# W1's loads in one queue, real B transposed and used first, the last 64 features in groups of 1,024 tokens, and the last columns in smaller pieces

## The chip, the cores and the metric

The kernel runs on one core of one Trainium2 chip. The metric is device time of one execution in microseconds (us). The execution's span in the trace is about 2 us shorter than that time; where a trace is read below, its span is quoted. All inputs are bf16.

## The reference

For x of 2,048 tokens by 640, the output is `g * a + (1 - g) * b`. `g` is a sigmoid gate per token, `a` is a diagonal state-space layer with 640 complex states, and `b` is a two-layer perceptron with 1,728 hidden features.

```python
Bu = einsum("bld,pd->blp", x, B_bar)              # B is complex: two real 640 x 640 matrices
for t in range(L):
    h = Lam_bar * h + Bu[:, t]                    # linear recurrence over the tokens
a = 2.0 * einsum("blp,dp->bld", hseq, C).real + x * Dskip     # C is complex too
b = gelu(x @ w1 + b1) @ w2 + b2                   # w1: 640 x 1728, w2: 1728 x 640
g = sigmoid((x * gate_w).sum(-1, keepdims=True))
```

The hidden features are 13 blocks of 128 and a last block of 64. That last block is one subject of the change.

## The kernel before

The tokens go in four quarters of 512. For each quarter TensorE does a hidden layer (`m1`), a B projection (`bproj`), then for each chunk of 128 tokens a second layer (`m2`) and a C projection (`cproj`). VectorE runs the recurrence as a scan, ScalarE does Gelu and takes results out of PSUM. Each engine's order comes from a small list scheduler inside the kernel, which uses estimated durations.

The first W1 columns come through the sync engine's queue (SPq), the rest in two loads from ScalarE's queue. The ten DMA transposes of B alternate between the real and the imaginary matrix and share one name, `"BT"`, so that the first projection waits for all ten:

```python
w1_rest(0, FW, NW2 * 128, "dtb")      # ScalarE's queue, 480 KB, after the first Exp
...
w1_rest(1, NW2 * 128, F, "sin")       # ScalarE's queue, 560 KB, after the sines
...
load_T("B", "l_B", [(BT[:, k, ci, :], (A_B_re, A_B_im)[ci][:, k * 128:(k + 1) * 128]) for k in range(KD) for ci in range(2)],
       ["BT"], prio=6.8, dur=13.1)
...
def bproj(q):
    for k in range(KP):
        for ci in range(2):           # real, imaginary, real, ...
            ...
            op(f"b_{q}_{k}{ci}", "pe", KD * d_mm(512), XT[q] + ["BT"], [("bank", bank)], f_mm, prio=pe_prio())
```

The last 64 features use half of the array's columns, so two halves of the quarter's tokens go to the two column halves, in every quarter:

```python
for k in range(KD):
    ...
    for h in range(2):                # n = 64 weights columns, 256 tokens each
        t = nc.tensor.matmul(PS[bank][h * 64:h * 64 + n, 0:256], W1sb[:, k, jf * 128:jf * 128 + n],
                             xT[:, k, q * 512 + h * 256:q * 512 + (h + 1) * 256], start=(k == 0), stop=(k == KD - 1))
```

The last chunk's C projection is two halves of 320 columns; after each, one VectorE operation adds everything up, and the half is stored.

## Time and profile before

218.64 us was the median of three runs (217.53 to 218.73).

| what | before |
|---|---|
| span of the traced run | 216.6 us |
| TensorE, VectorE, ScalarE busy | 98%, 88%, 46% |
| granted clock | 1.00 |
| chain from the first B projection to the last matmul | 21.70 to 213.92 us, TensorE alone |

The page's busy shares and its slices (40 equal slices of 5.4 us; a digit is the busy share in tenths) show an engine that is full and a DMA that is full only at the start:

```profile
PE 212.3 (98%) x1299; PEld 124.2 (57%) x1299; DVE 191.3 (88%) x268; ACT 100.2 (46%) x173; POOL 4.8 (2%) x14
...
PE   7999999999999999999999999999999999999995
...
DMA  6999499986300040000000013000000000000001
```

The chain of work that ended last, in order of time (start, us, what), follows the DMA issues on SPq, then the landing of the last imaginary transpose, then TensorE without a break:

```profile
16.75 4.91 DMA BT<-in_A_B_im_dram
21.66 0.05 issue
21.70 10.97 PE ps L690 x50
32.67 14.03 PE ps L658 x65
46.70 0.67 PE ps L662 x10
47.36 10.90 PE ps L690 x50
58.26 3.81 PE ps L765 x28
62.07 2.72 PE ps L789 x20
...
109.20 0.67 PE ps L662 x10
109.86 3.92 PE ps L765 x28
...
211.19 2.73 PE ps L789 x20
...
213.95 0.55 DVE osb L822
```

Three things are to be seen. 128x512 matmuls come every 216 ns (14.03 us / 65) and 128x320 ones every 136 ns (3.81 / 28). Each group of ten 64-column matmuls (line L662) takes 0.67 us, and the group after it is 0.11 us longer than its like elsewhere (3.92 against 3.81). And the first B projection (L690) starts on a DMA, not on TensorE. TensorE's own timeline shows the head and the hole there (start, duration, what, idle before it and what ended it):

```profile
5.17 0.94 PE L418 MATMUL ps<-ident,xn 128*128 128x128 bf16 x10
...
6.16 3.20 PE L637 MATMUL ps<-xT,W1sb 128*128 128x512 bf16 x14
...
20.52 0.74 PE L662 MATMUL ps<-xT,W1sb 128*64 128x256 bf16 x10
21.70 10.54 PE L690 MATMUL ps<-xT,BT 128*128 128x512 bf16 x48 [0.45 <-DMA BT<-in_A_B_im_dram]
```

### The profile page before, as it was taken

The numbers are of one execution on the slowest core, as the hardware profiler recorded it, in microseconds if no ns is written. First come the engines' busy times: TensorE is split into PE (matmuls) and PEld (weight loads), VectorE is DVE, ScalarE is ACT, GpSimd is POOL, SyncE is SP. The second block draws the span as 40 slices with busy tenths as digits, with TensorE's granted clock in tenths as the row PEclk, the third lists the DMA queues.
The fourth block names the chain that finished last, engine by engine and source line by source line (L and its number), as shares of the span: only waits on it lengthen the run. The fifth ranks groups of instructions, "written<-read, shape, count | busy, mean of one in ns | idle before, by whom it ended". The sixth has DMA issues, their size and how long they took to land.

```text
span 216.6 us, 3320 instructions
## 1 busy us (share of the span) xinstructions
PE 212.3 (98%) x1299; PEld 124.2 (57%) x1299; DVE 191.3 (88%) x268; ACT 100.2 (46%) x173; POOL 4.8 (2%) x14
## 2 busy tenths in 40 slices
PE   7999999999999999999999999999999999999995
PEld 3444444444577776444467777444457777777773
DVE  3899999999999999999997999799999989996312
ACT  2578556675533324556643233556673233232220
POOL 1010030000000100000000010000000000000000
PEclk9999999999999999999999999999999999999999
DMA  6999499986300040000000013000000000000001
GB/s 197 288 277 100 99 323 286 194 130 125 80 3 30 30 154 0 30 0 0 3 0 9 25 44 140 30 3 0 0 3 0 30 33 0 30 30 33 30 32 30
DMA packets 28858, 15.45 MB, mean 71 GB/s; under 512 B 22060, under 2 KB 28396, under 8 KB 28844
## 3 DMA queue, kind: packets, MB, share of 16 engines
q1 hardware_dynamic: 26912, 11.88, 23.5%
q0 software_dynamic: 560, 2.30, 3.5%
q10 hardware_dynamic: 1372, 1.07, 1.7%
q8 instruction: 10, 0.16, 0.3%
q14 instruction: 4, 0.03, 0.0%
HBM read 7.38 MB, written 2.62 MB: 46 GB/s over the span
## 4 chain that ended last, share of the span: by engine, by line
PE 89%; SPq 7%; DMA 2%; issue 0%; DVE 0%
PE ps L765 28%; PE ps L789 20%; PE ps L690 20%; PE ps L658 19%; SPq L335 6%; DMA BT<-in_A_B_im_dram 2%; SPq L328 1%; PE ps L662 1%; DVE osb L822 0%
## 5 line engine op out<-in xcount | busy, mean ns | idle before, releaser
L765 PE MATMUL ps<-W2sb,Gl 128*128 128x320 bf16 x448 | 63.6, 299 | 0.0
L765 PEld LDWEIGHTS ps<-W2sb,Gl 128*128 128x128 bf16 x448 | 43.6, 98 | 17.6 <-issue 0.4
L658 PE MATMUL ps<-xT,W1sb 128*128 128x512 bf16 x225 | 49.2, 379 | 0.0
L789 PE MATMUL ps<-CT,H 128*128 128x320 bf16 x320 | 46.1, 299 | 0.0
L730 DVE TENSOR_TENSOR_SCAN W<-atab,V 128x1280 bf16<-128x1280 f32 x16 | 44.3, 2812 | 0.3
L690 PE MATMUL ps<-xT,BT 128*128 128x512 bf16 x200 | 43.8, 379 | 0.4 <-DMA BT<-in_A_B_im_dram 0.4
L789 PEld LDWEIGHTS ps<-CT,H 128*128 128x128 bf16 x320 | 31.2, 98 | 12.3
L671 ACT ACTIVATE Gl<-ps,b1col 128x512 bf16<-128x512 f32 x45 | 30.6, 692 | 16.1 <-PE ps L658 16.1
L658 PEld LDWEIGHTS ps<-xT,W1sb 128*128 128x128 bf16 x225 | 22.0, 98 | 26.5
L690 PEld LDWEIGHTS ps<-xT,BT 128*128 128x128 bf16 x200 | 19.4, 98 | 23.7 <-DMA BT<-in_A_B_im_dram 0.7
L699 ACT ACTIVATE U<-ps 128x512 bf16<-128x512 f32 x40 | 23.9, 597 | 19.1 <-PE ps L690 19.1
L808 DVE SCALAR_TENSOR_TENSOR xg<-xn,gcol,dsk 128x640 bf16<-128x640 bf16 x16 | 13.9, 883 | 0.4
L773 ACT ACTIVATE E_0<-ps,g1col 128x320 bf16<-128x320 f32 x12 | 6.3, 527 | 16.5 <-PE ps L765 16.5
L616 DVE SCALAR_TENSOR_TENSOR scr<-xn,gwb 128x640 bf16<-128x640 bf16 x16 | 13.2, 823 | 0.4
L506 DVE TENSOR_TENSOR V<-V,W 128x1280 bf16<-128x1280 bf16 x16 | 12.5, 822 | 0.3
L506 DVE TENSOR_TENSOR H<-H,V 128x1280 bf16<-128x1280 bf16 x16 | 12.5, 822 | 0.3
L506 DVE TENSOR_TENSOR V<-mr,U 128x2560 bf16<-128x2560 bf16 x8 | 11.9, 1489 | 0.5 <-DVE s L506 0.3
L506 DVE TENSOR_TENSOR H<-c,W 128x2560 bf16<-128x2560 bf16 x8 | 11.9, 1488 | 0.1
L506 DVE TENSOR_TENSOR W<-mi,U 128x2560 bf16<-128x2560 bf16 x8 | 11.9, 1485 | 0.0
L506 DVE TENSOR_TENSOR V<-s,W 128x2560 bf16<-128x2560 bf16 x8 | 11.9, 1484 | 0.0
L773 ACT ACTIVATE E_2<-ps,g1col 128x320 bf16<-128x320 f32 x10 | 5.3, 527 | 13.4 <-PE ps L765 13.4
L773 ACT ACTIVATE E_1<-ps,g1col 128x320 bf16<-128x320 f32 x10 | 5.3, 528 | 13.3 <-PE ps L765 13.3
(95 smaller groups left out, 113.8 us busy)
## 6 DMA issues: line engine op xcount, KB each, us to landing
out_dram<-osb SPq DMA_DIRECT2D x15, 160.0 KB, 1.8
W2sb<-in_B_w_dram SPq DMA_DIRECT2D x1, 2080.0 KB, 12.7
xn<-in_A_x_dram POOLq DMA_DIRECT2D x3, 640.0 KB, 4.7
W1sb<-in_B_w_dram SPq DMA_DIRECT2D x5, 224.0 KB, 4.6
xn<-in_A_x_dram SPq DMA_DIRECT2D x2, 320.0 KB, 3.3
W1sb<-in_B_w_dram ACTq DMA_DIRECT2D x1, 560.0 KB, 5.2
W1sb<-in_B_w_dram ACTq DMA_DIRECT2D x1, 480.0 KB, 6.2
xT<-in_A_x_dram SPq DMA_TRANSPOSE x10, 4.0
```

Of the source, the lines that this page charges most:

```text
L335: t = dma_inc("sp", nc.sync.dma_start_transpose(dst, src), sem)
L506: return inc("dve", nc.vector.tensor_tensor(out=o, in0=a, in1=b, op=o_))
L616: t = inc("dve", nc.vector.scalar_tensor_tensor(out=scr[:, :], in0=xn[q % 2][:, c, :], scalar=1.0, in1=gwb[:, :], op0=ALU.mult, op1=ALU.mu ...
L658: t = nc.tensor.matmul(PS[bank][:, :], W1sb[:, k, jf * 128:(jf + 1) * 128], xT[:, k, q * 512:(q + 1) * 512], start=(k == 0), stop=(k == KD ...
L671: return inc("act", nc.scalar.activation(Gl[q % 2][:, jf, :], PS[bank][:, :], ACT.Gelu_apprx_tanh, bias=b1col[:, jf:jf + 1]))
L690: t = nc.tensor.matmul(PS[bank][:, :], BT[:, kd, ci, k * 128:(k + 1) * 128], xT[:, kd, q * 512:(q + 1) * 512], start=(kd == 0), stop=(kd = ...
L699: return inc("act", nc.scalar.activation(dst, src, ACT.Copy, scale=1.0 if ci == 0 else -1.0))
L730: t = inc("dve", nc.vector.tensor_tensor_scan(out=g[:, ci, :], data0=a, data1=v[:, ci, :], initial=0.0, op0=ALU.mult, op1=ALU.add))
L765: t = nc.tensor.matmul(PS[bank][:, 0:HALF], Gl[q % 2][0:n, jf, t4 * 128:(t4 + 1) * 128], W2sb[0:n, jf, cols], start=(jf == 0), stop=(jf == ...
L773: return inc("act", nc.scalar.activation(E1[c % NE][:, cols], PS[bank][:, 0:HALF], ACT.Copy, scale=g1col[:, c:c + 1]))
L789: t = nc.tensor.matmul(PS[bank][:, 0:HALF], H[b % NHB][:, ci, k, s * 128:(s + 1) * 128], CT[:, k, ci, cols], start=(i == 0), stop=(i == 2 ...
L808: return inc("dve", nc.vector.scalar_tensor_tensor(out=xg[c % 2][:, :], in0=xn[q % 2][:, c % 4, :], scalar=gcol[:, c:c + 1], in1=dsk[:, :] ...
```

## The change

The intent: TensorE is the bound, so take away its wait for B, make the 64-column groups fewer, and shorten what comes after the last matmul. The diff, cut to its core; left out are buffers, the banks' rotation, the second layer's last matmul reading the new buffer `GlL`, and the renaming of dependencies.

```diff
+        load("w1_r", "sp", "l_w1r", W1sb[:, :, FW:F], B_w1[:, FW:F].rearrange(...), [("w1", "r")], prio=6.5, lat=6.0)
...
-        w1_rest(0, FW, NW2 * 128, "dtb")
-        w1_rest(1, NW2 * 128, F, "sin")
...
-        load_T("B", "l_B", [(BT[:, k, ci, :], ...) for k in range(KD) for ci in range(2)], ["BT"], prio=6.8, dur=13.1)
+        for ci in range(2):
+            load_T(f"B{ci}", f"l_B{ci}", [(BT[:, k, ci, :], ...) for k in range(KD)], [("BT", ci)], prio=6.8 + 0.1 * ci, dur=6.6)
...
         def bproj(q):
-            for k in range(KP):
-                for ci in range(2):
+            for ci in range(2):
+                for k in range(KP):
...
+        def m1_last(q0):                      # the last 64 features of quarters q0 and q0 + 1
...
+                for k in range(KD):
+                    for h in range(2):
+                        t = nc.tensor.matmul(PS[bank][h * 64:(h + 1) * 64, :], W1sb[:, k, jf * 128:F],
+                                             xT[:, k, (q0 + h) * 512:(q0 + h + 1) * 512], start=(k == 0), stop=(k == KD - 1))
...
+        LAST = [(BK_C[0], 0, HALF), (BK_C[1], HALF, HALF + 192), (BK_M2[0], HALF + 192, D)]
...
         m1(1)
+        m1_last(0)
...
             m1(q)
+            if q % 2 == 0:
+                m1_last(q)
```

More of the change, by code (lines that the diff above doesn't have):

```diff
@@ L236, in bass_gated_mix__ssm_conv_s5__dense_activation_gelu__prompt_kernel @@
         CT = SB("CT", [128, KP, 2, D], BF16)
-        Gl = [SB(f"Gl_{i}", [128, NF, 512], BF16) for i in range(2)]
+        Gl = [SB(f"Gl_{i}", [128, NF - 1, 512], BF16) for i in range(2)]
+        GlL = [SB(f"GlL_{i}", [65, 512], BF16) for i in range(3)]
         dsk = SB("dsk", [128, D], BF16)
@@ L348, in bass_gated_mix__ssm_conv_s5__dense_activation_gelu__prompt_kernel @@
         FW = NW * 128
-        NW2 = 10
         for k in range(KD):
@@ L352, in bass_gated_mix__ssm_conv_s5__dense_activation_gelu__prompt_kernel @@
                  [("w1", k)], prio=2 + k, lat=2.6 + 0.2 * k)
+        load("w1_r", "sp", "l_w1r", W1sb[:, :, FW:F], B_w1[:, FW:F].rearrange("(k p) f -> p k f", p=128), [("w1", "r")], prio=6.5, lat=6.0)
         nmain = (NF - 1) * 128
@@ L397, in f_ones @@
         def f_ones():
-            inc("dve", nc.vector.memset(Gl[0][64:65, NF - 1, :], 1.0))
-            return inc("dve", nc.vector.memset(Gl[1][64:65, NF - 1, :], 1.0))
+            t = None
+            for i in range(3):
+                t = inc("dve", nc.vector.memset(GlL[i][64:65, :], 1.0))
+            return t
         op("ones", "dve", 1.1, (), ["gl1"], f_ones, prio=-40)
@@ L475, in bass_gated_mix__ssm_conv_s5__dense_activation_gelu__prompt_kernel @@
         op("amag", "act", 0.3, ["acol"], ["amag"], f_amag, prio=-949)
-        def w1_rest(i, f0, f1, key):
-            load(f"w1_r{i}", "act", f"l_w1r{i}", W1sb[:, :, f0:f1], B_w1[:, f0:f1].rearrange("(k p) f -> p k f", p=128), [("w1", ("ra", "rb")[i])],
-                 prio=-949.5, lat=4.0, reads=[key])
-        w1_rest(0, FW, NW2 * 128, "dtb")
         ang, psi, sh, sq, kf = tr
@@ L592, in bass_gated_mix__ssm_conv_s5__dense_activation_gelu__prompt_kernel @@
                    [("xT", q) for q in range(a, e)], prio=6 + a, dur=4.4 * (e - a))
-        load_T("B", "l_B", [(BT[:, k, ci, :], (A_B_re, A_B_im)[ci][:, k * 128:(k + 1) * 128]) for k in range(KD) for ci in range(2)],
-               ["BT"], prio=6.8, dur=13.1)
+        for ci in range(2):
+            load_T(f"B{ci}", f"l_B{ci}", [(BT[:, k, ci, :], (A_B_re, A_B_im)[ci][:, k * 128:(k + 1) * 128]) for k in range(KD)],
+                   [("BT", ci)], prio=6.8 + 0.1 * ci, dur=6.6)
         load("w2a", "sp", "l_w2a", W2sb[:, 0:NF - 1, :], B_w2[0:nmain, :].rearrange("(j p) d -> p j d", p=128), ["w2a"], prio=7.5, lat=8.0)
@@ L604, in in_bank @@
             ctr["in"] += 1
-            return (7 + i) % 8 if i < 2 * (NF + 2 * KP) - NW else BK_IN[i % 4]
+            return (7 + i) % 8 if i < 2 * (NF - 1 + 2 * KP) + 1 - NW else BK_IN[i % 4]
         def pe_prio():
@@ L649, in m1, with f_mm @@
         def m1(q, j0=0):
-            for jf in range(j0, NF):
+            for jf in range(j0, NF - 1):
                 bank = in_bank()
-                n = 128 if jf < NF - 1 else FL
-                def f_mm(jf=jf, bank=bank, n=n):
+                def f_mm(jf=jf, bank=bank):
                     t = None
                     for k in range(KD):
-                        if n == 128:
-                            t = nc.tensor.matmul(PS[bank][:, :], W1sb[:, k, jf * 128:(jf + 1) * 128], xT[:, k, q * 512:(q + 1) * 512],
-                                                 start=(k == 0), stop=(k == KD - 1))
-                            continue
-                        for h in range(2):
-                            t = nc.tensor.matmul(PS[bank][h * 64:h * 64 + n, 0:256], W1sb[:, k, jf * 128:jf * 128 + n],
-                                                 xT[:, k, q * 512 + h * 256:q * 512 + (h + 1) * 256], start=(k == 0), stop=(k == KD - 1))
-                    return inc("pe", t)
-                op(f"m1_{q}_{jf}", "pe", KD * d_mm(512 if n == 128 else 256) + (0.0 if n == 128 else 0.15),
-                   XT[q] + ([("w1", k) for k in range(KD)] if jf < NW else [("w1", "rb" if jf >= NW2 else "ra")]), [("bank", bank)], f_mm, prio=pe_prio())
-                def f_ge(jf=jf, bank=bank, n=n):
-                    if n == 128:
-                        return inc("act", nc.scalar.activation(Gl[q % 2][:, jf, :], PS[bank][:, :], ACT.Gelu_apprx_tanh, bias=b1col[:, jf:jf + 1]))
-                    t = None
-                    for h in range(2):
-                        ph = slice(h * 64, h * 64 + n)
-                        t = inc("act", nc.scalar.activation(Gl[q % 2][0:n, jf, h * 256:(h + 1) * 256], PS[bank][ph, 0:256],
-                                                            ACT.Gelu_apprx_tanh, bias=b1col[ph, jf:jf + 1]))
-                    return t
-                op(f"ge_{q}_{jf}", "act", d_act(512) if n == 128 else 2 * d_act(256), [("bank", bank), "b1col"], [("gl", q % 2, jf)], f_ge, prio=10)
@@ new lines, in f_mm, with f_ge @@
+                        t = nc.tensor.matmul(PS[bank][:, :], W1sb[:, k, jf * 128:(jf + 1) * 128], xT[:, k, q * 512:(q + 1) * 512],
+                                             start=(k == 0), stop=(k == KD - 1))
+                    return inc("pe", t)
+                op(f"m1_{q}_{jf}", "pe", KD * d_mm(512), XT[q] + ([("w1", k) for k in range(KD)] if jf < NW else [("w1", "r")]),
+                   [("bank", bank)], f_mm, prio=pe_prio())
+                def f_ge(jf=jf, bank=bank):
+                    return inc("act", nc.scalar.activation(Gl[q % 2][:, jf, :], PS[bank][:, :], ACT.Gelu_apprx_tanh, bias=b1col[:, jf:jf + 1]))
@@ new lines, in m1, with f_mm, f_ge @@
+                op(f"ge_{q}_{jf}", "act", d_act(512), [("bank", bank), "b1col"], [("gl", q % 2, jf)], f_ge, prio=10)
+        def m1_last(q0):
+            jf = NF - 1
+            bank = in_bank()
+            def f_mm():
+                t = None
+                for k in range(KD):
+                    for h in range(2):
+                        t = nc.tensor.matmul(PS[bank][h * 64:(h + 1) * 64, :], W1sb[:, k, jf * 128:F],
+                                             xT[:, k, (q0 + h) * 512:(q0 + h + 1) * 512], start=(k == 0), stop=(k == KD - 1))
+                return inc("pe", t)
+            op(f"m1_{q0}_{jf}", "pe", KD * d_mm(512) + 0.2, XT[q0] + XT[q0 + 1] + [("w1", "r")], [("bank", bank)], f_mm, prio=pe_prio())
+            def f_ge():
+                t = None
+                for h in range(2):
+                    ph = slice(h * 64, (h + 1) * 64)
+                    t = inc("act", nc.scalar.activation(GlL[(q0 + h) % 3][0:64, :], PS[bank][ph, :], ACT.Gelu_apprx_tanh, bias=b1col[ph, jf:jf + 1]))
+                return t
+            op(f"ge_{q0}_{jf}", "act", 2 * d_act(512), [("bank", bank), "b1col"], [("glL", q0 % 3), ("glL", (q0 + 1) % 3)], f_ge, prio=10)
@@ L692, in f_mm @@
                         return inc("pe", t)
-                    op(f"b_{q}_{k}{ci}", "pe", KD * d_mm(512), XT[q] + ["BT"], [("bank", bank)], f_mm, prio=pe_prio())
+                    op(f"b_{q}_{k}{ci}", "pe", KD * d_mm(512), XT[q] + [("BT", ci)], [("bank", bank)], f_mm, prio=pe_prio())
                     def f_ev(k=k, ci=ci, bank=bank):
@@ L762, in f_mm @@
                     t = None
-                    for jf in range(NF):
-                        n = 128 if jf < NF - 1 else FL + 1
-                        t = nc.tensor.matmul(PS[bank][:, 0:HALF], Gl[q % 2][0:n, jf, t4 * 128:(t4 + 1) * 128], W2sb[0:n, jf, cols],
-                                             start=(jf == 0), stop=(jf == NF - 1))
+                    ts = slice(t4 * 128, (t4 + 1) * 128)
+                    for jf in range(NF - 1):
+                        t = nc.tensor.matmul(PS[bank][:, 0:HALF], Gl[q % 2][:, jf, ts], W2sb[:, jf, cols], start=(jf == 0), stop=False)
+                    t = nc.tensor.matmul(PS[bank][:, 0:HALF], GlL[q % 3][0:FL + 1, ts], W2sb[0:FL + 1, NF - 1, cols], start=False, stop=True)
                     return inc("pe", t)
-                op(f"m2_{c}_{hf}", "pe", NF * d_mm(HALF), [("gl", q % 2, jf) for jf in range(NF)] + ["gl1", "w2a", "w2b", "b2"],
+                op(f"m2_{c}_{hf}", "pe", NF * d_mm(HALF), [("gl", q % 2, jf) for jf in range(NF - 1)] + [("glL", q % 3), "gl1", "w2a", "w2b", "b2"],
                    [("bank", bank)], f_mm, prio=pe_prio())
@@ L775, in m2, with f_mm @@
                 op(f"e1_{c}_{hf}", "act", d_act(HALF), [("bank", bank), ("g", q)], [("E1", c % NE, hf)], f_ev, prio=5)
+        LAST = [(BK_C[0], 0, HALF), (BK_C[1], HALF, HALF + 192), (BK_M2[0], HALF + 192, D)]
         def cproj(c):
             q, b, s = c // 4, c // 2, c % 2
-            for hf in range(2):
-                bank = BK_C[hf]
-                cols = slice(hf * HALF, (hf + 1) * HALF)
-                def f_mm(bank=bank, cols=cols):
+            pieces = LAST if c == NCH - 1 else [(BK_C[hf], hf * HALF, (hf + 1) * HALF) for hf in range(2)]
+            for hf, (bank, c0, c1) in enumerate(pieces):
+                cols = slice(c0, c1)
+                def f_mm(bank=bank, cols=cols, n=c1 - c0):
                     t = None
@@ L788, in f_mm @@
                         for ci in range(2):
-                            t = nc.tensor.matmul(PS[bank][:, 0:HALF], H[b % NHB][:, ci, k, s * 128:(s + 1) * 128], CT[:, k, ci, cols],
+                            t = nc.tensor.matmul(PS[bank][:, 0:n], H[b % NHB][:, ci, k, s * 128:(s + 1) * 128], CT[:, k, ci, cols],
                                                  start=(i == 0), stop=(i == 2 * KP - 1))
@@ L792, in f_mm @@
                     return inc("pe", t)
-                op(f"c_{c}_{hf}", "pe", 2 * KP * d_mm(HALF), [("H", b % NHB), "CT"], [("bank", bank)], f_mm, prio=pe_prio())
+                op(f"c_{c}_{hf}", "pe", 2 * KP * d_mm(c1 - c0), [("H", b % NHB), "CT"], [("bank", bank)], f_mm, prio=pe_prio())
                 if c == NCH - 1:
@@ L817, in comb, with f_fin, f_st @@
                 op("last", "dve", d_dve(D, 2), [("xg", c % 2), ("E1", c % NE, 0), ("E1", c % NE, 1)], [("E2", c % NE, 0), ("E2", c % NE, 1)], f_half, prio=-50)
-                for hf in range(2):
-                    cols = slice(hf * HALF, (hf + 1) * HALF)
-                    def f_fin(hf=hf, cols=cols):
-                        return inc("dve", nc.vector.scalar_tensor_tensor(out=osb[c % NO][:, cols], in0=PS[BK_C[hf]][:, 0:HALF], scalar=gcol[:, c:c + 1],
+                for i, (bank, c0, c1) in enumerate(LAST):
+                    cols = slice(c0, c1)
+                    def f_fin(bank=bank, cols=cols, n=c1 - c0):
+                        return inc("dve", nc.vector.scalar_tensor_tensor(out=osb[c % NO][:, cols], in0=PS[bank][:, 0:n], scalar=gcol[:, c:c + 1],
                                                                         in1=E2[c % NE][:, cols], op0=ALU.mult, op1=ALU.add))
-                    op(f"fin{hf}", "dve", d_dve(HALF), [("bank", BK_C[hf]), ("E2", c % NE, hf)], [("osb", c % NO, hf)], f_fin, prio=-60)
-                    def f_st(hf=hf, cols=cols):
-                        return dma_inc("sp", nc.sync.dma_start(o2[c * 128:(c + 1) * 128, cols], osb[c % NO][:, cols]), f"stl{hf}")
-                    op(f"stl{hf}", "sp", 0.5, [("osb", c % NO, hf)], [], f_st, prio=1000 + c, lat=2.5)
+                    op(f"fin{i}", "dve", d_dve(c1 - c0), [("bank", bank), ("E2", c % NE, min(i, 1))], [("osb", c % NO, i)], f_fin, prio=-60)
+                    if i == 1:
+                        continue
+                    def f_st(i=i, cols=slice(0, HALF) if i == 0 else slice(HALF, D)):
+                        return dma_inc("sp", nc.sync.dma_start(o2[c * 128:(c + 1) * 128, cols], osb[c % NO][:, cols]), f"stl{i}")
+                    op(f"stl{i}", "sp", 0.5, [("osb", c % NO, j) for j in ((0,), (), (1, 2))[i]], [], f_st, prio=1000 + c, lat=2.5)
                 return
@@ L838, in comb @@
             op(f"cmb{c}", "dve", 2 * d_dve(D, 2), [("xg", c % 2)] + [(e, c % NE, hf) for e in ("E1", "E2") for hf in range(2)],
-               [("osb", c % NO, 0), ("osb", c % NO, 1)], f_cmb, prio=-50)
+               [("osb", c % NO, 0), ("osb", c % NO, 1), ("osb", c % NO, 2)], f_cmb, prio=-50)
             def f_st():
                 return dma_inc("sp", nc.sync.dma_start(o2[c * 128:(c + 1) * 128, :], osb[c % NO][:, :]), f"st{c % NO}")
-            op(f"st{c}", "sp", 0.5, [("osb", c % NO, 0), ("osb", c % NO, 1)], [], f_st, prio=1000 + c, lat=2.5)
+            op(f"st{c}", "sp", 0.5, [("osb", c % NO, 0), ("osb", c % NO, 1), ("osb", c % NO, 2)], [], f_st, prio=1000 + c, lat=2.5)
         def outs(q):
@@ L912, in final_sp @@
                 nc.sync.wait_ge(sems[f"st{i}"], E.count[f"st{i}"])
-            for hf in range(2):
+            for hf in (0, 2):
                 nc.sync.wait_ge(sems[f"stl{hf}"], E.count[f"stl{hf}"])
```

## The prediction

> **What bounds the kernel.** TensorE. On the page it is busy 98% of the 216.6 us span (VectorE 88%, ScalarE 46%), granted clock 1.00. The chain of waits is TensorE without a break from 21.70 to 213.92 us: 128x512 matmuls every 216 ns (65 in 14.03 us), 128x320 ones every 136 ns (28 in 3.81 us). The only large hole is 0.45 us at 21.25, where the first B projection waits for the last transpose of imaginary B (timeline).
>
> **1. B transposes, real first.** Today all ten must land (21.66 us) before the first B projection; the DMA engines are full until then (slices of the page). The real half alone should land at about 16 to 17 us, against a need at 20.5; the imaginary half still at about 22, against 20.5 + 25 x 0.216 = 25.9. The hole closes: -0.45 us, all on the critical path.
>
> **2. W1 in one queue.** The later loads leave ScalarE's queue; 1,040 KB now stand ahead of the transposes. First use is at 13.95 us. Up to its end 320 + 1,120 + 1,040 KB must pass; at the 300 GB/s of the windows from 2 to 12 us that is done at 10 to 11 us. W1 caused no wait before: 0. The transposes of x for the second quarter move 0.45 us later; they landed at about 27.5 and are needed at about 31.3: 0.
>
> **3. Last 64 features for 1,024 tokens at once.** Four visits of ten 64-column matmuls (N = 256, in pairs on two halves of the array) take 0.67 us each in the chain, and what follows is 0.11 us longer than its like (10.90 against 10.79, 3.92 against 3.81). Five pairs at N = 256 need 5 x 0.107 = 0.54, so each visit pays about 0.24 us for entering and leaving the mode. The Trainium skill (TensorEngine Tiling (Array Packing), Key Properties) says that changing the tiling mode drains the engine; the 0.24 us agree. After: two visits of 5 x 0.216 + 0.24 = 1.32, together 2.64 in place of 3.12: -0.48 us.
>
> **4. Last columns in pieces.** Ten matmuls of 320 columns (1.36 us) become ten of 192 and ten of 128. The 128-column transposes of x come every 80 ns here ((0.94 - 0.22)/9), and the skill (TensorE: Matmul & The Clock Gate, Back-to-back issue gap) gives about 81 ns for N = 128. With 82 ns for 192 columns: 1.63 us, +0.27. The last VectorE operation shrinks from 0.55 to about 0.35 us, the last matmul's latency by 0.08. Net about 0.
>
> **VectorE** has slack (at the end it waits 4.6 us for ScalarE): no TensorE wait for H expected.
>
> **Sum:** 218.64 - 0.45 - 0.48 = 217.7; with runs of before from 217.53 to 218.73, I say 217.6, range 216.8 to 218.4, -0.5%: within 2% at 0.96, faster 0.02, slower 0.02.
>
> **What would show it.** The wait for B at 21.25 gone; two 64x512 groups of about 1.2 us, and 0.11 us once after each; 128-column matmuls 80 ns apart, the last VectorE operation about 0.35 us; TensorE's busy time about 0.5 us lower.
>
> **What would make it wrong.** The rest of W1 landing after 13.95 us (a TensorE hole there); the real half later than 20.5; 64-column pairs not overlapping at N = 512 (each visit 2.2 us: +2 in all); a changed VectorE order that makes TensorE wait for H.

## The result, and the profile after

The changed kernel took 217.87 us (median of 6 runs, 217.37 to 218.03), the kernel before 218.55 us (6 runs, 217.53 to 218.73). The ratio is 0.9974 with a 95% interval of 0.9952 to 0.9996: within 2%, and just clear of 1. A ratio here is the mean time of one kernel's fast runs over that of the other's of the same rounds, so it is not quite the ratio of the medians. The prediction (217.6, range 216.8 to 218.4) holds it; but that range holds every gain from 0.15 to 1.75 us on 218.55, so the time alone tests little.

The first line of the page after. TensorE's busy time fell by 0.6 us (212.3 to 211.7):

```profile
PE 211.7 (98%) x1289; PEld 124.0 (58%) x1289; DVE 191.8 (89%) x270; ACT 99.3 (46%) x169; POOL 4.8 (2%) x14
```

The chain of work that ended last, after. Apart from a memset in front of it, it is TensorE's own work now, from 1.20 us to 212.89 (shown from the first B projection on):

```profile
20.52 10.79 PE ps L699 x50
31.31 14.03 PE ps L654 x65
45.34 1.20 PE ps L675 x10
46.54 10.90 PE ps L699 x50
...
108.38 1.20 PE ps L675 x10
109.58 1.87 PE ps L774 x13
...
210.13 2.76 PE ps L800 x30
212.89 0.03 issue
212.91 0.35 DVE osb L833
```

TensorE's timeline after, at the head:

```profile
6.10 3.20 PE L635 MATMUL ps<-xT,W1sb 128*128 128x512 bf16 x14
...
20.36 10.96 PE L699 MATMUL ps<-xT,BT 128*128 128x512 bf16 x50
```

There is no wait for B. There are two 64-column groups of 1.20 us in place of four of 0.67. The last thirty matmuls (320, 192 and 128 columns) take 2.76 us in place of 2.73 for twenty, and the last VectorE operation takes 0.35 in place of 0.55.

The two spans differ by 1.2 us (216.6 and 215.4), the means of the timed runs by 0.57 (0.26% of 218.55). So the pair of traces tells twice as much as the timing. That gap became the main question: which of the 1.2 us is there in every execution?

### The profile page after: what moved, and what is told of

Its sections match the earlier page's. It is cut to its first block, busy times and chain, and to the rows that moved or that the text cites. A ratio compares the mean times of both kernels' runs of the same rounds, so it can differ in the third digit from the quotient of the medians.

```text
span 215.4 us, 3296 instructions
## 1 busy us (share of the span) xinstructions
PE 211.7 (98%) x1289; PEld 124.0 (58%) x1289; DVE 191.8 (89%) x270; ACT 99.3 (46%) x169; POOL 4.8 (2%) x14
## 4 chain that ended last, share of the span: by engine, by line
PE 98%; DVE 0%; issue 0%
PE ps L774 26%; PE ps L654 23%; PE ps L800 20%; PE ps L699 20%; PE ps L635 4%; PE ps L775 2%; PE ps L393 1%; PE ps L675 1%; PE ps L421 1%; DVE osb L833 0%; DVE wz L386 0%; PE ps L410 0%; PE ps L441 0%; PE ps L453 0%
## 5 line engine op out<-in xcount | busy, mean ns | idle before, releaser
L774 PE MATMUL ps<-W2sb,Gl 128*128 128x320 bf16 x416 | 61.4, 299 | 0.0
L774 PEld LDWEIGHTS ps<-W2sb,Gl 128*128 128x128 bf16 x416 | 40.6, 98 | 16.6 <-issue 0.4
L800 PE MATMUL ps<-CT,H 128*128 128x320 bf16 (+2 forms) x330 | 46.1, 295 | 0.0
L800 PEld LDWEIGHTS ps<-CT,H 128*128 128x128 bf16 x330 | 31.7, 98 | 12.0
L654 PEld LDWEIGHTS ps<-xT,W1sb 128*128 128x128 bf16 x225 | 22.1, 98 | 26.5
L708 ACT ACTIVATE U<-ps 128x512 bf16<-128x512 f32 x40 | 23.9, 597 | 18.3 <-PE ps L699 18.3
```

Source lines behind the costliest of these rows:

```text
L654: t = nc.tensor.matmul(PS[bank][:, :], W1sb[:, k, jf * 128:(jf + 1) * 128], xT[:, k, q * 512:(q + 1) * 512], start=(k == 0), stop=(k == KD ...
L708: return inc("act", nc.scalar.activation(dst, src, ACT.Copy, scale=1.0 if ci == 0 else -1.0))
L774: t = nc.tensor.matmul(PS[bank][:, 0:HALF], Gl[q % 2][:, jf, ts], W2sb[:, jf, cols], start=(jf == 0), stop=False)
L800: t = nc.tensor.matmul(PS[bank][:, 0:n], H[b % NHB][:, ci, k, s * 128:(s + 1) * 128], CT[:, k, ci, cols], start=(i == 0), stop=(i == 2 * K ...
```

## The experiments

Each run gives one trace and up to six times. The parts of the change are called A (real B first), B (W1 in one queue), C (last 64 features in pairs of quarters) and D (last columns in pieces). The edits shown are cut to their core (`...` marks a cut). The theory at the outset was the prediction's: A is worth 0.45 us, C 0.48, B and D nothing. The main rivals were that moving W1 is what closes the hole, and that the 64-column groups were slow for their weight loads, not for the switch.

### e1: A alone

```diff
-        load_T("B", ... for k in range(KD) for ci in range(2)], ["BT"], ...)
+        for ci in range(2):
+            load_T(f"B{ci}", ... for k in range(KD)], [("BT", ci)], ...)
...
-            for k in range(KP):
-                for ci in range(2):
+            for ci in range(2):
+                for k in range(KP):
```

> The kernel before with only the B part of the change: real B transposed first, used first, its own semaphore. Theory (the hole at 21.25 us was the wait for the tenth transpose): the 0.45 us hole is gone and nothing else moves; span 0.45 us shorter than before, time ratio about 0.998. Rival (the hole was DMA contention from W1 arriving in ScalarE's queue beside the transposes, and only moving W1 closes it): a hole before the first B projection stays, ratio 1.000.

Measured: 218.10 us (217.74 to 220.40, 6 runs), ratio 1.0006 (0.9971 to 1.0041). The trace has no wait for B; its span is 215.8 us, 0.8 less than that of the first trace of before. But this trace doesn't show what A does. Its last transpose of B was issued at 16.95 us and landed 4.0 us later, at 20.9, just as TensorE reached the projection (20.93): there would have been next to no wait without A either. In the changed kernel's trace A is at work: the projection starts at 20.36, and the last transpose of B, issued at 19.40, lands 4.5 us later, at about 23.9. First e1's, then the changed kernel's:

```profile
L335 SPq DMA_TRANSPOSE BT<-in_A_B_im_dram x1: 1272/1272/1272, 16.9 to 16.9; - x1
...
DMA to landing us min/median/max: 4.0/4.0/4.0
```

```profile
L336 SPq DMA_TRANSPOSE BT<-in_A_B_im_dram x1: 1270/1270/1270, 19.4 to 19.4; - x1
...
DMA to landing us min/median/max: 4.5/4.5/4.5
```

That A is enough without moving W1 is shown by e8 below. The timed runs of e1 do not show 0.45 us; one of the six, 220.40 us, weighs on them (the mean is 218.46 with it and 218.07 without, against 218.29 for before).

### e2: B alone

```diff
-        w1_rest(0, ...)
-        w1_rest(1, ...)
+        load("w1_r", "sp", "l_w1r", W1sb[:, :, FW:F], ..., prio=6.5, lat=6.0)
```

> The kernel before with only W1's rest moved into the sync queue in front of the ten interleaved B transposes. Theory (1,040 KB ahead push the transposes later, and all ten are needed): the tenth lands at 22.8 to 23.7 us in place of 21.66, the hole grows from 0.45 to 1.6 to 2.5 us, time ratio 1.005 to 1.010. Rival (moving W1 is what closed the hole): the hole is gone, ratio 0.998. W1 itself causes no wait in either.

Measured: 219.96 us (219.62 to 222.50), ratio 1.0105 (1.0064 to 1.0147), slightly over the range expected. Two of the six runs (221.84 and 222.50 us) had a lower granted clock, 0.992; the other four alone average 219.85, 0.7% above before, inside the range. TensorE's timeline shows the hole grown from 0.45 to 1.52 us (1.6 to 2.5 was expected):

```profile
20.88 0.74 PE L656 MATMUL ps<-xT,W1sb 128*64 128x256 bf16 x10
23.14 10.96 PE L684 MATMUL ps<-xT,BT 128*128 128x512 bf16 x50 [1.52 <-DMA BT<-in_A_B_im_dram]
```

The rival is dead: W1 in front of the transposes makes them later (the tenth landed at 23.08 us), and it is A that makes this harmless: the changed kernel has W1 in the same place and no wait.

### e3: C alone

```diff
-                        for h in range(2):       # in m1, every quarter: 256 tokens to each half
+        m1_last(q0)                              # after quarters 1 and 2: 512 tokens to each half
```

> The kernel before with only the last 64 features computed for 1,024 tokens at once (two visits in place of four). Theory: visits 4 x 0.78 = 3.12 us become 2 x 1.31 = 2.62 us, -0.50 us. The first visit moves from 20.5 to after the second quarter's matmuls, so TensorE reaches the B projection 0.74 us earlier and waits for B's tenth transpose longer: hole 0.45 + 0.74 = 1.19 us. So alone it should give only 0.50 - 0.00 net of -0.50 + (hole grows 0.74, the visit's 0.78 having left that place and 0.53 paid later): net about +0.24 us, ratio 1.001. Rival (savings of the parts simply add): -0.50 us, ratio 0.998.

The arithmetic in that text is muddled in the middle; its claim is a net of +0.24 us, ratio 1.001. Measured: 217.87 us, ratio 0.9977 (0.9957 to 0.9997). That is a miss. In the trace the chain after the first B projection is 0.28 us longer than in before, as it should be (195.18 against 194.90 us to the end), but the hole is 0.41 us and not 1.19: TensorE had started its first W1 matmul 0.44 us later than in before (6.60 against 6.16), and B's tenth transpose had landed earlier (21.37 against 21.66). This pointed to the head as the thing that varies.

### e4: D alone

```diff
+        LAST = [(BK_C[0], 0, HALF), (BK_C[1], HALF, HALF + 192), (BK_M2[0], HALF + 192, D)]
```

> The kernel before with only the last half of the columns in pieces of 192 and 128. Theory from the trace of after: 20 matmuls take 1.40 us in place of 1.36 for ten, last VectorE operation 0.35 in place of 0.55, span 0.2 us shorter, ratio 0.999. Rival (as I predicted, a floor of about 80 ns for 128 columns): 1.63 us, net 0.

Measured: 218.23 us (fast runs 217.83 to 218.24), ratio 0.9990 (0.9969 to 1.0011), which cannot tell 0.2 us from 0. The traced run was slow (225.64 us, clock 0.949), so its trace says nothing about this. D's size is read below from the tails of the fast traces.

### e5: the same two visits with twice as many matmuls of half the length

```diff
-                for k in range(KD):
-                    for h in range(2):           # N = 512
+                for s in range(2):
+                    for k in range(KD):
+                        for h in range(2):       # N = 256
```

> The changed kernel, but in each of the two visits for the last 64 features twenty matmuls of N = 256 in place of ten of N = 512. Theory (a visit pays a fixed price for entering and leaving the half-array mode, whatever is done in it): a visit takes 10 x 0.107 + 0.13 = 1.20 us in the chain, as in the changed kernel, and 0.11 us after it; time as the changed kernel. Rival (the old N = 256 matmuls were slow one by one, for weight loads that don't hide: 0.67 us for five pairs = 0.134 us a pair): 1.34 us a visit, +0.28 us in all.

Measured: 217.87 us, ratio 0.9984 (0.9962 to 1.0006). The chain decides:

```profile
46.83 1.21 PE ps L677 x20
```

Twenty matmuls of N = 256 take 1.21 us, ten of N = 512 took 1.20. The rival (1.34 us) falls: the short matmuls are not slow one by one, and the price is paid once for a visit.

### e6: one visit for all 2,048 tokens

```diff
+                    if (q, ci, k) == (1, 1, 2):
+                        m1_last(0)
+                        m1_last(2)
...
-        m1_last(0)                               # after m1(1)
-                m1_last(q)                       # after m1(2)
```

> The changed kernel, with the last 64 features of all 2,048 tokens in one visit of twenty matmuls of N = 512, between two blocks of the second quarter's B projection. Theory (fixed price of a visit, 0.13 inside and 0.11 after it): one visit of 10 x 0.216 + 0.13 = 2.29 us and 0.11 after it, 2.40 in place of 2 x 1.31 = 2.62: the chain is 0.22 us shorter than the changed kernel's. Rival (no fixed price): 2 x 1.31 = 2.62, no change.

Measured: 217.59 us (217.43 to 217.77), ratio 0.9968 (0.9954 to 0.9981). In the chain the visit is 2.30 us. What follows is fifteen matmuls in 3.33 us (0.14 + 3.19; one record is missing, which the chain shows as an "issue"; the trace holds 196 of this line's 200 matmuls). That is 0.09 longer than 15 x 0.216. Together the visit costs 2.39 us, where 2.40 was expected:

```profile
53.47 2.30 PE ps L675 x20
55.77 0.14 issue
55.91 3.19 PE ps L702 x14
```

The span from the first W1 matmul to the end is 209.0 us against 209.3 in the changed kernel: 0.27 us shorter, where 0.22 was expected (e10 below, with the same single visit, has 209.1: 0.20 shorter).

### e7: last pieces of 256 and 64 columns

```diff
-        LAST = [..., (BK_C[1], HALF, HALF + 192), (BK_M2[0], HALF + 192, D)]
+        LAST = [..., (BK_C[1], HALF, HALF + 256), (BK_M2[0], HALF + 256, D)]
```

> The changed kernel with last pieces of 256 and 64 columns in place of 192 and 128. Theory A (a matmul costs its columns over 2.4 GHz plus about 3 ns, weight loads hidden): ten of 64 take 0.30 us, the thirty last matmuls 2.75 us in the chain as before (2.76), the last VectorE operation 0.29 in place of 0.35 us: span 0.06 us shorter. Theory B (a floor of about 50 ns or more for each matmul with its own weights, so that 64 columns cost as much as 128): thirty take 2.95 us or more, span 0.15 us or more longer.

Measured: 217.61 us, ratio 0.9972 (0.9954 to 0.9990). In the chain twenty matmuls (320 and 256 columns) take 2.47 us; TensorE's last matmul ends at 212.97, so the ten of 64 columns took 212.97 - 210.22 - 2.47 = 0.28 us, 28 ns each:

```profile
210.22 2.47 PE ps L800 x20
212.68 0.02 issue
212.71 0.48 DVE osb L833
213.19 0.19 DVEq L226
```

Theory A's matmul cost is right and a floor of 50 ns is ruled out. The cost itself can be worked out from the trace of before: (215.8 - 136.1) / (512 - 320) = 0.415 ns for a column, which is 2.4 columns in a ns, and 3 ns are left over; for 64 columns that makes 30 ns. Its conclusion was still wrong: the span did not shrink by 0.06, because the 256-column VectorE operation is still running when the last matmul ends. From the first C matmul to the last VectorE end it is 3.17 us here, 3.13 with 192 and 128, and 3.31 in before.

This trace has something more: TensorE waited for the last transpose of C, in the middle of the kernel. It is taken up under point 2 below.

### e8: the changed kernel without B

```diff
-        load("w1_r", "sp", ...)
+        w1_rest(0, FW, NW2 * 128, "dtb")
+        w1_rest(1, NW2 * 128, F, "sin")
```

> The changed kernel with W1's rest back in two loads from ScalarE's queue. Theory (W1 in one queue is worth nothing once real B comes first): no TensorE hole appears at 13.9, 17 or 20.5 us, the chain after 20.5 us is the same, time as the changed kernel within 0.1%; the x transposes of the second quarter land at about 27.3 us in place of 29.8, against a need at 31.2. Rival (it is what made the transposes early enough): a hole before the first or the sixth block of the B projection.

Measured: 217.29 us (216.93 to 219.59), ratio 0.9972 (0.9937 to 1.0007). No hole appears, though the last transpose of B, issued at 17.52, landed 4.2 us later, at 21.7, after TensorE's arrival (20.52): with A and without B the late half costs nothing. The span from the first W1 matmul is 209.3 us, as with B. The landing of the second quarter's x transposes can be read from the GpSimd load that waits for them and starts about 0.3 us after it. First the changed kernel, then e8:

```profile
29.80 0.57 POOL L329 DMA_DIRECT2D dsk<-in_A_Dskip_dram  x1 [16.10 <-DMA xT<-in_A_x_dram]
```

```profile
27.50 0.57 POOL L329 DMA_DIRECT2D dsk<-in_A_Dskip_dram  x1 [13.63 <-DMA xT<-in_A_x_dram]
```

So B buys no time that these runs show, and costs 2.3 us of slack. It does so in all fast traces: this load starts at 26.3 to 27.8 us in the seven without B and at 29.0 to 30.4 in the six with it.

### e11, e12: before and e3 once more

Nothing is edited; these two are second traces, to see whether the hole is a constant.

> The kernel before once more, for a second trace. Theory (the wait for B in the kernel before is what is left of the tenth transpose's landing after TensorE's own head, whose first W1 matmul started anywhere from 5.9 to 7.6 us in the traces so far): hole = landing less (start of the first W1 matmul + 15.1), or 0; if the start is 6.6 or later there is little or no hole and the span is start + 210.0. Rival (the hole is a fixed 0.45 us): 0.45 us whatever the start.

> The kernel of e3 once more, because its timed runs (ratio 0.9977) were better than the +0.24 us that its trace explains. Theory (the landing of the tenth transpose varies from execution to execution, and the profiled one was a late one): from the first B projection on the chain is again 0.28 us longer than before's; the hole is landing less (start + 14.4) or 0. If the landing is 20.6 us or earlier, the span is start + 209.5; the ratio is again between 0.997 and 1.001. Rival (something else in it is faster): the chain after the first B projection is shorter than 195.18 us.

The kernel before, again (217.76 us, one run): TensorE's timeline has no wait for B at all.

```profile
5.91 3.18 PE L637 MATMUL ps<-xT,W1sb 128*128 128x512 bf16 x14
...
20.25 0.74 PE L662 MATMUL ps<-xT,W1sb 128*64 128x256 bf16 x10
20.92 10.97 PE L690 MATMUL ps<-xT,BT 128*128 128x512 bf16 x50
```

C alone, again: 218.27 us (217.47 to 219.08), ratio 1.0000 (0.9974 to 1.0026), and a hole three times that of e3.

```profile
6.39 3.18 PE L640 MATMUL ps<-xT,W1sb 128*128 128x512 bf16 x14
...
22.10 10.97 PE L704 MATMUL ps<-xT,BT 128*128 128x512 bf16 x50 [1.31 <-DMA BT<-in_A_B_im_dram]
```

The rival "a fixed 0.45 us" falls. The same program had a hole of 0.45 us in one execution and none in another, and e3's program 0.41 and 1.31. The tenth transpose landed by 20.92 in one and at about 22.1 in another. Also the start of the first W1 matmul does not settle it alone: the earliest start (5.91) had no hole. Both ends of the race move. The chain after the first B projection was 195.2 us in both traces of C alone, so nothing hidden in C is faster, and its first ratio (0.9977) was probably a lucky draw of the head; the two intervals overlap.

### e13, e10: the changed kernel once more, and the parts that help put together

```diff
+        # e10 = e8 (W1's rest on ScalarE's queue) with e6's single visit;
+        # the fourth memset of ones waits for the identity matrix
+        op("ones3", "dve", 0.5, ["ident"], ["gl13"], f_ones3, prio=-40)
```

> The changed kernel on the same chip as e10, for comparison. Theory: span less start of the first W1 matmul again 209.3 us, no TensorE wait for B whatever the start, ratio to before 0.996 to 0.998.

> The best parts together: the changed kernel with all last 64 features in one visit (as e6) and W1's rest on ScalarE's queue (as e8), and the fourth memset of ones after the identity matrix, which e6's four memsets had pushed from 3.39 to 3.93 us. Theory: span less the start of the first W1 matmul is 209.0 us, as in e6 (changed kernel 209.3, before 210.4); time 0.25 us below the changed kernel of the same chip. If the savings don't add, 209.3.

On one chip: e13 217.62 us (217.30 to 218.26), ratio 0.9974 (0.9951 to 0.9997), the same as the first time; e10 217.37 us (216.80 to 217.53), ratio 0.9953 (0.9931 to 0.9974). From the first W1 matmul to the end e13 has 209.3 us and e10 209.1. The intervals of the two overlap, so the times alone don't prove e10 faster than the changed kernel; the chain does show a shorter TensorE program, and e10 has the lowest ratio of all versions tried (e8's median, 217.29 us, is lower, but on another chip and with a ratio of 0.9972). e10's six-run mean is 0.19% below e13's.

### All fast traces side by side

The starts are from TensorE's timeline; the last two columns are worked out from the span (span less start). e11 is a single run; its clock is 1.00.

| trace | first W1 matmul | wait for B | first B matmul | span | from first W1 matmul | from first B matmul |
|---|---|---|---|---|---|---|
| before | 6.16 | 0.45 | 21.70 | 216.6 | 210.4 | 194.9 |
| e11, before again | 5.91 | none | 20.92 | 215.8 | 209.9 | 194.9 |
| e1, A | 5.92 | none | 20.93 | 215.8 | 209.9 | 194.9 |
| e2, B | 6.52 | 1.52 | 23.14 | 218.0 | 211.5 | 194.9 |
| e3, C | 6.60 | 0.41 | 21.42 | 216.6 | 210.0 | 195.2 |
| e12, C again | 6.39 | 1.31 | 22.10 | 217.3 | 210.9 | 195.2 |
| after | 6.10 | none | 20.36 | 215.4 | 209.3 | 195.0 |
| e13, after again | 6.21 | none | 20.48 | 215.5 | 209.3 | 195.0 |
| e5 | 7.61 | none | 21.85 | 216.9 | 209.3 | 195.1 |
| e6 | 6.67 | none | 20.93 | 215.7 | 209.0 | 194.8 |
| e7 | 5.89 | none | 20.15 | 215.5 | 209.6 | 195.4 |
| e8 | 6.25 | none | 20.52 | 215.5 | 209.3 | 195.0 |
| e10 | 6.41 | none | 20.67 | 215.5 | 209.1 | 194.8 |

The first W1 matmul starts anywhere from 5.89 to 7.61 us, a range larger than the change. Two traces of one program differ by 0.11 to 0.25 us here. The late one, e5, was that program's slowest run (218.72 us, the other three 217.39 to 217.97), so it is taken as chance and not as e5's edit; a second trace of e5 was not taken. The sixth column takes that noise out: with real B first it is 209.3 in the changed kernel's traces, and 209.9 in before when B happens not to be late.

## Why the prediction was right, point by point

The time was right (217.6 predicted, 217.87 measured), and the sum of the gain nearly so: -0.93 us predicted, -0.57 measured. The terms were less good than the sum; two errors of opposite sign, the hole's and the last columns', partly cancelled. That part of the closeness is luck.

**1. The hole, "-0.45 us, all on the critical path": mechanism right, size wrong.** The failed step is taking one execution's wait for the program's. The hole is a race between the landing of the tenth transpose and TensorE's arrival: 0.45 us in one trace of before, none in the other. e1, with A alone, measured 1.0006 (0.9971 to 1.0041), so A's worth in the mean is not resolved and may be near 0. The intervals can't decide it: that of the changed kernel allows a gain from 0.09 to 1.05 us. What A does give is certainty: none of the eight fast traces with real B first waits for B (in e1's and e10's there was next to nothing to wait for), while the trace with B and without A waited 1.52 us, and those with C and without A 0.41 and 1.31. C needs A: it brings TensorE to the B projection 0.75 us sooner.

**2. W1 in one queue, "0": right for the time, wrong about the slack.** e8 undoes it and loses nothing. The second quarter's x transposes were put at 0.45 us later; they landed 2.3 us later (29.80 against 27.51 in before), against a need at 31.15. The imaginary half of B was put at about 22 us and landed at about 23.9, against a need at 25.8 (20.36 + 25 x 0.216). And a delay at the head of a queue was handed down it. The last transpose of C was issued at 54.90 us in before and at 56.93 after (53.7 to 55.5 in the seven fast traces without B, 56.0 to 58.0 in the six with it). The first C projection, which needs it, started at 61.91 in the first trace of before, 61.12 in the second and 61.09 after: the need did not move back with the transfer. I had not looked that far. In e7, whose loads are the changed kernel's, this reserve ran out. The sync queue's and TensorE's timelines of e7:

```profile
57.78 1.27 SPq L336 DMA_TRANSPOSE CT<-in_A_C_im_dram  x1
```

```profile
60.74 0.30 PE L775 MATMUL ps<-W2sb,GlL 65*128 65x320 bf16 x1
61.17 2.08 PE L800 MATMUL ps<-CT,H 128*128 128x320 bf16 x14
```

In the chain that ended last, the step before the C matmul is that transfer, and not TensorE:

```profile
57.78 3.34 DMA CT<-in_A_C_im_dram
```

The C matmul follows 0.43 us after its predecessor's start, where the changed kernel has 0.14 (60.95 to 61.09); this 0.29 us is why e7's last column is 195.4. With W1 on ScalarE's queue the last C transpose is issued at 55.42 against a need at 61.25 in e8, and at 53.69 against 62.48 in e10.

**3. The 64-column groups, "-0.48 us": right, and shown.** In the table, C takes TensorE to the first B matmul 0.75 us sooner (14.26 against 15.01 us after the first W1 matmul, in after and e11) and costs 0.28 later: -0.47. That the price is for the visit and not for the matmuls is shown by e5 (20 short matmuls cost what 10 long ones do) and e6 (one visit fewer saves another 0.27; 0.20 in e10). The Trainium skill (TensorEngine Tiling (Array Packing), Key Properties) says that a change of tiling mode drains TensorE; about 0.24 us for a visit is what this case shows of it. That it is the drain itself, and not something else at the switch, is argued, not shown.

**4. The last columns, "net about 0": wrong by 0.18 us.** The failed step is "+0.27" for the matmuls. I took 80 ns for 128 columns from a group of transposes in the trace of before, and found it confirmed by the 81 ns of the Trainium skill (TensorE: Matmul & The Clock Gate, Back-to-back issue gap). But that group of ten took 0.94 us there and 0.73 in others (e1, e3, e8, e11), which is (0.73 - 0.22) / 9 = 57 ns (0.22 us is the record of one transpose). The one that I read changed its pace in the middle: its matmuls start at 5.17, 5.25, 5.35, 5.46, 5.57, 5.67 and then 5.72, 5.78, 5.83, 5.89, so 80 ns is the mean of two paces, and its agreement with 81 was chance. The thirty last matmuls cost 2.76 us against 2.73, not 0.27 more. The last VectorE operation was foreseen rightly (0.35). From the first C matmul to the last VectorE end it is 3.13 us after and 3.31 before, so D gives -0.18.

So what every execution gains is C and D, -0.47 - 0.18 = -0.65 us by the chain, against 209.9 - 209.3 = 0.6 in the table and 0.57 in the mean times.

**VectorE** made TensorE wait for no H, in any trace, as predicted.

## What to carry to other kernels

A wait in one trace is a sample, not a constant: before counting on it, ask whether both sides of the race, the transfer and the engine that needs it, move from run to run, and take a second trace of the old kernel. That a wait is gone from one trace proves as little: see whether the transfer still lands late there. When a load is moved to the front of a queue, follow the delay to the queue's end and set each later transfer against its need in the changed kernel. Switching the array to half-width cost about 0.24 us each time here, so collect such work into few visits; and shorter pieces at the end pay only until the next engine in the chain becomes the one that is late.

## What the Trainium skill lacked or had wrong

- TensorE: Matmul & The Clock Gate, Back-to-back issue gap: it gives about 81 ns (N = 128) and 131 ns (N = 512) for streams of weight loads and matmuls, and offers N/2.4 + 2.5 ns for an isolated one. The streams here, each matmul with its own weights, follow the isolated formula: 215.8 ns at 512 columns (14.03 us / 65), 136 at 320 (3.81 / 28), 57 at 128 (transposes after the start, e11), 28 at 64 (e7). No floor showed down to 64 columns.
- The same page, What's actually happening, says that the array's clock opens after about 3.4 us of activity and that the moment varies from run to run. The traces agree that there is such a change and that its moment varies: transposes go from one every 107 ns to one every 56 ns between 3.2 us (e11) and about 5 us (e10) after TensorE's first matmul. So the second group of ten took 0.73 us in some executions and 1.25 in others (e5, e10), and in the trace of before a weight load of this kind took 97 to 152 ns. The granted clock in the page's slices does not show it. What the page lacks is the effect on comparing kernels: together with other waits of the head, the first W1 matmul started between 5.89 and 7.61 us, which is more than this change is worth.
- TensorEngine Tiling (Array Packing), Key Properties: it says that a mode switch drains TensorE and gives no number. Here a visit to the 64-column mode cost about 0.24 us beyond its matmuls (0.67 + 0.11 - 0.54), and one visit fewer saved 0.27 (e6) and 0.20 (e10).
- No page that I found says how much a DMA transpose's landing varies: the tenth transpose of B landed by 20.92 us in one execution of the kernel before and at 21.66 in another.
